# Decode attention with an MLP gate on one core: double K turns, one softmax pass per unit, and 640 rows of wo on eight partitions at a time

## The chip, the cores and the metric

The kernel runs on one core of a Trainium2 chip. The metric is the device time of one execution in microseconds (us). The core has five engines with their own instruction streams: TensorE (PE, matrix products; its weight loads are shown as PEld), VectorE (DVE), ScalarE (ACT), GpSimd (POOL) and SyncE (SP, which here only issues DMAs). Sixteen DMA engines move data between HBM and the on-chip memory SBUF. TensorE writes its results to PSUM.

## What is computed

One token of a decoder for a batch of two. Attention reads a cache of 32,768 keys and values for each of two sequences and eight KV heads; four query heads share one KV head. The attention output is projected by `wo` and multiplied by a gate that a small MLP makes from the same input.

```python
xn = layernorm(x)                                  # x: 2 x 1 x 512
q = (xn @ wq).reshape(B, 1, 32, 128)               # wq: 512 x 4096
scores = einsum("bhqd,bhkd->bhqk", q, k) * 128**-0.5   # K: 2 x 8 x 32768 x 128, bf16
p = softmax(scores)
o = einsum("bhqk,bhkd->bhqd", p, v)                # V: the same size as K
s = o.reshape(B, 1, 4096) @ wo                     # wo: 4096 x 512
h2 = gelu(layernorm(xn) @ w3) @ w4                 # the one token makes the rest of the MLP's
g = silu(xn + h2)                                  # first block zero
out = x + s * g
```

K and V together are 268 MB. Each element is used once or four times, so the kernel has to read all of it and does little with it.

## The kernel before

**Loads.** All large inputs go through five SBUF slots of 4 MB (`slots`, SLOTS = 5) in the order of the list `loads`: the first K chunk, wq, the second K chunk, w3, w4, and then K of unit n+1 and V of unit n by turns. A unit is one (sequence, KV head) pair; there are 16 units, and each has two K chunks and two V chunks (`NCH` = 2) of 16,384 rows. A chunk is one DMA of 128 partitions with 32 KB each. The main loop (line 441) walks the list, does the job of entry i, and then calls `issue(i + SLOTS)`, which starts the load five entries ahead on SP's queue. SP waits there until the slot is free. The last four entries are pieces of wo with 16, 8, 4 and 4 of the 32 rows that each partition holds (`wo_cuts`). The last V chunk is cut into two DMAs.

**K job** (`k_job`, line 295). A chunk is cut into eight blocks of 16 x 128 keys (`GT` = 16). For each block `transposed` turns 128 x 1024 words of 32 bits on VectorE in squares of 32 into a buffer `ktb` (`KTB` = 3 buffers), and `scores` then does four matmuls of 512 columns on the turned block. `scores` runs one block behind the turning (`LAG` = 1). The scores of a unit stand in two PSUM tiles `sc`, one for each half.

**Softmax.** After the last block of a half VectorE takes the maximum of that half (line 239), and after the second half the maximum of the two. The closures `step1` and `step2` are put on the list `glue` and run one after the other between later blocks: `step1` brings the maximum across partitions, `step2` does the exponential, its sum and a transposition (`pT`), each once per half.

**V job** (`v_job`, line 307). Each chunk takes 32 matmuls of 512 columns in four column strips of TensorE, all adding into `acc`. After a unit's last V chunk `unit_end` copies `acc` to SBUF, and its `step1` adds the four strips by `sel` in four fp32 products (`ot`, line 342), and writes the normalised output into `oQ` by four VectorE instructions of 32 partitions, so that one transposition (`oP`, line 354) has it ready for wo after the last head.

**wo job** (`wo_job`, line 358). For each of the 32 rows r of a partition it does four matmuls of 128 columns into four strips of `s_ps`, 128 matmuls in all. Two VectorE instructions (lines 458 and 460) then apply the gate and add x, and two DMAs store the result.

The instructions of each engine stand in the order in which the code issues them (`manual_schedule`); the framework adds the semaphore waits. The DMAs that SP issues use eight completion semaphores in rotation, and a DMA waits until the one eight places earlier has landed.

Of the kernel before, what the change touches and what calls it, by code (L numbers as in the profile page):

```python
# [8 lines left out]
F32 = mybir.dt.float32  # L9
BF16 = mybir.dt.bfloat16  # L10
U32 = mybir.dt.uint32
ACT = mybir.ActivationFunctionType
ALU = mybir.AluOpType
# [4 lines left out]
SLOTS = 5  # L18
KTB = 3
LAG = 1  # L20
# [3 lines left out]
def kernel(  # L24
# [44 lines left out]
    p_pool = ctx.enter_context(tc.tile_pool(name="prob", bufs=2))  # L69
    pt_pool = ctx.enter_context(tc.tile_pool(name="probT", bufs=4))  # L70
    tmp = ctx.enter_context(tc.tile_pool(name="tmp", bufs=3))
    sm_pool = ctx.enter_context(tc.tile_pool(name="small", bufs=3))
    sc_psp = ctx.enter_context(tc.tile_pool(name="sc_ps", bufs=4, space=bass.MemoryType.PSUM))
    acc_psp = ctx.enter_context(tc.tile_pool(name="acc_ps", bufs=1, space=bass.MemoryType.PSUM))
# [7 lines left out]
    NR = HD // 128  # L82
    wo_v = A_wo.rearrange("(p r) d -> p r d", r=NR)

# [3 lines left out]
    for n in range(NU):  # L88
        for c in range(NCH):
            if n + 1 < NU:  # L90
                loads.append(("K", n + 1, c))
            loads.append(("V", n, c))
    wo_cuts = [0, NR // 2, 3 * NR // 4, NR - 4, NR]
    loads += [("wo", r0, r1) for r0, r1 in zip(wo_cuts, wo_cuts[1:])]
    tiles = {}

    def issue(i):
        if i >= len(loads):
            return
        what = loads[i]  # L100
        t = slots.tile([128, UT * Dh], BF16, tag="slot", name=f"slot_{what[0]}")
        if what[0] in ("K", "V"):
            b, g = units[what[1]]
            c = what[2]
            src = A_k_cache if what[0] == "K" else A_v_cache
            sv = src[b, g, c * CH:(c + 1) * CH, :].rearrange("(p t) d -> p (t d)", p=128)
            w = UT * Dh // 2 if what == ("V", NU - 1, NCH - 1) else UT * Dh
            for w0 in range(0, UT * Dh, w):
                nc.sync.dma_start(out=t[:, w0:w0 + w], in_=sv[:, w0:w0 + w])
        elif what[0] == "wq":  # L110
            nc.sync.dma_start(
                out=t[:, 0:DK * HD].rearrange("p (k f) -> p k f", k=DK), in_=wq_v)
        elif what[0] == "wo":
            r0, r1 = what[1:]
            nc.sync.dma_start(
                out=t[:, 0:(r1 - r0) * D].rearrange("p (r d) -> p r d", d=D), in_=wo_v[:, r0:r1, :])
        elif what[0] == "w3":
            nc.sync.dma_start(
                out=t[:, 0:DK * Fdim].rearrange("p (k f) -> p k f", k=DK), in_=w3_v)
        else:  # L120
            nc.sync.dma_start(
                out=t[:, 0:FK * D].rearrange("p (f d) -> p f d", f=FK), in_=w4_v)
        tiles[what] = t
# [23 lines left out]
    for k in range(4):  # L147
        wb, par = k // 2, k % 2
        src = ident[:, :].rearrange("p (wb w two) -> p wb two w", wb=2, two=2)[:, wb, par, :]
        nc.vector.tensor_copy(out=pick[:, k, :, :], in_=src.unsqueeze(1).to_broadcast([128, 4, 32]))  # L150

    headm = pers.tile([128, rep], F32)
# [50 lines left out]
    oQ = pers.tile([128, B, NR], BF16)  # L203
    oP = pers.tile([128, B, NR], BF16)
    g_sb = pers.tile([B, D], F32)
# [8 lines left out]
    def state(n):  # L214
        if n not in unit_st:
            unit_st[n] = {
                "m2": sm_pool.tile([128, NHALF], F32, tag="m2", name="m2"),
                "sc": [], "pT": [],
            }
        return unit_st[n]  # L220

    def scores(n, grp, ktb):
        b, g = units[n]
        st = state(n)
        half, sl = grp // NS, grp % NS
        if sl == 0:
            st["sc"].append(sc_psp.tile([128, GT * 32], F32, tag="sc", name="sc"))
        sc = st["sc"][half]
        kv = ktb[:, :].bitcast(BF16).rearrange("p (t wb k two) -> p wb two t k", wb=2, k=32, two=2)
        off = 32 - rep - rep * sl  # L230
        for k in range(4):
            nc.tensor.matmul(  # L232
                sc[:, :].rearrange("p (t k) -> p t k", k=32),
                lhsT=qz[:, n % 2, k, off:off + 128],
                rhs=kv[:, k // 2, k % 2, :, :],
                start=(sl == 0 and k == 0), stop=(sl == NS - 1 and k == 3),
            )
        if sl == NS - 1:
            nc.vector.tensor_reduce(out=st["m2"][:, half:half + 1], in_=sc[:, :], axis=AX.X, op=ALU.max)  # L239
            if half == NHALF - 1:  # L240
                softmax_front(n)

    def softmax_front(n):
# [3 lines left out]
        m1 = sm_pool.tile([128, 1], F32, tag="m1", name="m1")  # L247
        nc.vector.tensor_reduce(out=m1[:, :], in_=st["m2"][:, :], axis=AX.X, op=ALU.max)  # L248

# [11 lines left out]
        def step2():  # L261
# [5 lines left out]
            nc.vector.tensor_scalar_mul(out=nb[:, :], in0=bc[:, :], scalar1=-inv_sqrt_dh)  # L267
            S2 = sm_pool.tile([128, NHALF], F32, tag="S2", name="S2")
            for hf in range(NHALF):
                pr = p_pool.tile([128, GT * 32], BF16, tag="p", name="pr")  # L270
                nc.scalar.activation(  # L271
                    out=pr[:, :], in_=st["sc"][hf][:, :], func=ACT.Exp,
                    bias=nb[:, 0:1], scale=inv_sqrt_dh, accum_out=S2[:, hf:hf + 1])
                pT = pt_pool.tile([128, GT, 32], BF16, tag="pT", name="pT")
                nc.vector.transpose(out=pT[:, :, :].rearrange("p t r -> p (t r)"), in_=pr[:, :])  # L275
                st["pT"].append(pT)
            S1 = sm_pool.tile([128, 1], F32, tag="S1", name="S1")
            nc.vector.reduce_sum(out=S1[:, :], in_=S2[:, :], axis=AX.X)
            Sm = sm_pool.tile([128, rep], F32, tag="Sm", name="Sm")
# [6 lines left out]
    def transposed(n, grp, kw):  # L286
        ktb = kt_pool.tile([128, GT * DW], U32, tag="ktb", name="ktb")
        nc.vector.transpose(out=ktb[:, :], in_=kw)  # L288
        waiting.append((n, grp, ktb))

    def flush(keep):
        while len(waiting) > keep:
            scores(*waiting.pop(0))

    def k_job(n, c):
        kw = tiles[("K", n, c)][:, :].bitcast(U32)
        for blk in range(NB):
            transposed(n, c * NB + blk, kw[:, blk * GT * DW:(blk + 1) * GT * DW])
            if n == 0 and c == 0 and blk < KTB:
                if blk == KTB - 1:  # L300
                    q_job()
                continue
            flush(LAG)
            if glue:
                glue.pop(0)()

    def v_job(n, c):
        vv = tiles[("V", n, c)][:, :].rearrange("p (e i t d) -> p e t i d", i=4, t=GT, d=Dh)
        for e in range(NB // 4):
            half, r0 = (c * NB + e * 4) // NS, (c * NB + e * 4) % NS * rep  # L310
            pT = unit_st[n]["pT"][half]
            for t in range(GT):
                j = t % 4
                nc.tensor.matmul(  # L314
                    acc[32 * j:32 * j + 16, :].rearrange("p (i d) -> p i d", d=Dh),
                    lhsT=pT[:, t, r0:r0 + 16],
                    rhs=vv[:, e, t, :, :],
# [14 lines left out]
    def unit_end(n):  # L332
# [5 lines left out]
        def step1():  # L338
# [7 lines left out]
            nc.vector.reciprocal(out=rc[:, :], in_=ot[:, rep:2 * rep])  # L346
            q0, c0 = g // 2 * 32, g % 2 * 4 * rep
            ov = oQ[q0:q0 + 32, b, c0:c0 + 4 * rep].rearrange("r (h a) -> r a h", a=4)
            for a in range(4):
                nc.vector.tensor_tensor(  # L350
                    out=ov[:, a, :], in0=ot[32 * a:32 * a + 32, 0:rep], in1=rc[32 * a:32 * a + 32, :],
                    op=ALU.mult)
            if g == Hkv - 1:
                nc.vector.transpose(out=oP[:, b, :], in_=oQ[:, b, :])

        glue.append(step1)

    def wo_job(r0, r1):
        w = tiles[("wo", r0, r1)]
        for r in range(r0, r1):  # L360
            for j in range(4):
                c0 = (r - r0) * D + 128 * j
                nc.tensor.matmul(
                    s_ps[32 * j:32 * j + B, :], lhsT=oP[:, :, r], rhs=w[:, c0:c0 + 128],
                    start=(r == 0), stop=(r == NR - 1), tile_position=(0, 32 * j))

# [74 lines left out]
    for i, what in enumerate(loads):  # L441
        if what[0] == "K":
            k_job(what[1], what[2])
        elif what[0] == "V":
            if what[2] == 0:
                while glue and len(unit_st[what[1]]["pT"]) < NHALF:
                    glue.pop(0)()
            v_job(what[1], what[2])
        elif what == ("w4",):
            mlp_job()  # L450
        elif what[0] == "wo":
            while glue:
                glue.pop(0)()
            wo_job(what[1], what[2])
        issue(i + SLOTS)
# [37 lines left out]
```

## Time and profile before

| | |
|---|---|
| median of 3 runs | 661.09 us (660.92 to 661.11) |
| profiled execution | 660.95 us, its span from first to last instruction 659.2 us |
| granted TensorE clock, mean | 0.794 of full speed |
| PE busy | 440.4 us (67%), 2594 matmuls |
| DVE busy | 391.0 us (59%), 551 instructions |
| ACT busy | 42.4 us (6%) |
| DMA | 280.89 MB, mean 426 GB/s; SP's queue 98.8% of 16 engines' span |
| K turns (line 288) | 256 instructions, 299.5 us, 1218 ns each |
| score matmuls (line 232) | 1024, 322.7 us, 461 ns each |
| V matmuls (line 314) | 1024, 68.9 us |

The page gives for each engine the time in which it was busy, a picture of the span in 40 slices, the DMA queues, the chain of waits that ended last, and the costliest groups of instructions. Windows of the trace give the same numbers for any stretch, with the granted clock and the share of the DMA engines that was busy; the timeline lists single instructions with what ended the idle time before them. Behind the DMA view the trace holds a record of every DMA packet with its start, duration, size and queue; it does not name the DMA engine.

### The profile page before, as it was taken

The page shows a single profiled execution, that of the slowest core. Times are in us where ns is not written, and L with a number is a line of the kernel's source. Part 1 is how long each engine was busy: PE and PEld are TensorE (multiplying, and loading weights), DVE is VectorE, ACT ScalarE, POOL GpSimd, SP SyncE. Part 2 cuts the span into 40 slices and gives each one's busy share as a digit, 9 for nine tenths or more (in the row PEclk, how much of TensorE's full clock was granted, in tenths as well). Part 3 has the DMA queues.
Part 4 walks back from the last instruction along what each step waited for, and adds up shares of the span by engine and source line. Part 5 has one row for each costly group of instructions (what it writes and reads, how often), then busy time and mean ns, then how long its engine had stood idle before and what let it go on. Part 6 is the DMA issues. An engine that isn't in the chain of part 4 may idle for free.

```text
span 659.2 us, 6264 instructions
## 1 busy us (share of the span) xinstructions
PE 440.4 (67%) x2594; PEld 183.1 (28%) x2594; DVE 391.0 (59%) x551; ACT 42.4 (6%) x136; POOL 2.2 (0%) x10
## 2 busy tenths in 40 slices
PE   0596968486685748757466885747678484965864
PEld 0342332132332213222122322213232221422233
DVE  6184957466664746657375765746576474666621
ACT  1103010000001000000100000000000000000000
POOL 1000000000000000000000000000000000000000
PEclk9997878879586886859788585977858788686976
DMA  9999999999999999999999999999999999999995
GB/s 382 420 436 439 427 437 430 430 442 420 440 430 430 440 424 436 435 425 439 427 435 435 424 442 428 431 439 425 437 433 429 441 423 436 430 430 440 430 422 245
DMA packets 10447, 280.89 MB, mean 426 GB/s; under 512 B 1194, under 2 KB 1204, under 8 KB 1460
## 3 DMA queue, kind: packets, MB, share of 16 engines
q1 hardware_dynamic: 10376, 280.50, 98.8%
q8 instruction: 20, 0.33, 0.2%
q14 instruction: 7, 0.06, 0.0%
q10 hardware_dynamic: 44, 0.01, 0.0%
HBM read 280.50 MB, written 0.00 MB: 426 GB/s over the span
## 4 chain that ended last, share of the span: by engine, by line
DMA 75%; PE 12%; DVE 8%; issue 4%; ACT 1%; SPq 0%; DVEq 0%; ACTq 0%
DMA slot_K<-in_A_k_cache_dram 39%; DMA slot_V<-in_A_v_cache_dram 30%; PE sc L232 7%; DVE ktb L288 6%; DMA slot_wq<-in_A_wq_dram 3%; PE acc L314 3%; DMA slot_wo<-in_A_wo_dram 2%; DVE pT L275 1%; PE h L425 1%; PE qT L372 1%; PE hT L405 1%; ACT pr L271 0%; DVE oQ L350 0%; PE ot L342 0%; PE bc L263 0%
## 5 line engine op out<-in xcount | busy, mean ns | idle before, releaser
L232 PE MATMUL sc<-ktb,qz 128*128 128x512 bf16 x1024 | 322.7, 461 | 169.9 <-DVE ktb L288 162.1
L288 DVE STREAM_TRANSPOSE ktb<-slot_K 128x1024 uint32<-128x1024 uint32 x256 | 299.5, 1218 | 121.2 <-DMA slot_K<-in_A_k_cache_dram 113.7
L232 PEld LDWEIGHTS <-qz 128*128 128x128 bf16 x1024 | 108.7, 112 | 350.8 <-issue 249.7
L314 PE MATMUL acc<-slot_V,pT 128*16 128x512 bf16 x1024 | 68.9, 391 | 13.9 <-DMA slot_V<-in_A_v_cache_dram 13.8
L239 DVE TENSOR_REDUCE m<-sc 128x1 f32<-128x512 f32 x32 | 22.1, 690 | 58.0 <-PE sc L232 58.0
L314 PEld LDWEIGHTS <-pT 128*16 128x16 bf16 x1024 | 24.0, 90 | 59.9 <-issue 40.0
L271 ACT ACTIVATE pr<-sc,nb 128x512 bf16<-128x512 f32 x32 | 21.7, 682 | 214.1 <-DVE nb L267 214.1
L396 ACT COPY qz<-qp 32x16 bf16<-32x16 bf16 x64 | 12.9, 201 | 343.2 <-PE sc L232 321.7
L275 DVE STREAM_TRANSPOSE pT<-pr 128x512 bf16<-128x512 bf16 x32 | 22.1, 711 | 14.4 <-ACT pr L271 14.4
L342 PE MATMUL ot<-sel,acs 128*128 128x4 f32 x128 | 25.5, 322 | 0.5 <-DVE acs L336 0.5
L342 PEld LDWEIGHTS ot<-sel,acs 128*128 128x128 f32 x128 | 24.9, 289 | 0.6 <-DVE acs L336 0.6
L336 DVE COPY acs<-acc 128x512 f32<-128x512 f32 x16 | 11.1, 692 | 17.6 <-PE acc L314 17.6
L372 PE MATMUL qT<-xT,slot_wq 128*128 128x2 bf16 x128 | 3.6, 165 | 12.4 <-DMA slot_wq<-in_A_wq_dram 12.4
L263 PEld LDWEIGHTS bc<-ones_f,gx 1*128 1x128 f32 x32 | 7.5, 291 | 13.4 <-issue 12.2
L350 DVE TENSOR_TENSOR oQ<-ot,rc 32x4 bf16<-32x4 f32 x64 | 10.5, 164 | 1.2
L267 DVE TENSOR_SCALAR nb<-bc 128x1 f32<-128x1 f32 x16 | 2.5, 155 | 14.5 <-PE bc L263 14.5
L340 PEld LDWEIGHTS ot<-Sm,ones_f 128*128 128x128 f32 x32 | 9.1, 291 | 6.2 <-issue 4.9
L263 PE MATMUL bc<-ones_f,gx 1*128 1x1 f32 x32 | 8.9, 344 | 1.1 <-DVE gx L257 1.1
L372 PEld LDWEIGHTS <-slot_wq 128*128 128x128 bf16 x128 | 3.5, 104 | 12.4 <-DMA slot_wq<-in_A_wq_dram 12.4
L346 DVE RECIPROCAL rc<-ot 128x4 f32<-128x4 f32 x16 | 2.4, 150 | 7.5 <-PE ot L342 7.5
L425 PE MATMUL h<-slot_w,h_bf 128*2 128x512 bf16 x14 | 5.4, 571 | 1.6 <-DVE h_bf L422 1.6
L252 PE MATMUL mT<-identf,m 128*1 128x128 f32 x16 | 4.3, 270 | 3.2 <-DVE m L248 3.2
(68 smaller groups left out, 69.0 us busy)
## 6 DMA issues: line engine op xcount, KB each, us to landing
slot_K<-in_A_k_cache_dram SPq DMA_DIRECT2D x32, 4096.0 KB, 40.0
slot_V<-in_A_v_cache_dram SPq DMA_DIRECT2D x31, 4096.0 KB, 34.0
slot_wq<-in_A_wq_dram SPq DMA_DIRECT2D x1, 4096.0 KB, 21.5
slot_V<-in_A_v_cache_dram SPq DMA_DIRECT2D x2, 2048.0 KB, 28.9
slot_w<-in_B_w_dram SPq DMA_DIRECT2D x2, 1792.0 KB, 39.2
slot_wo<-in_A_wo_dram SPq DMA_DIRECT2D x1, 2048.0 KB
slot_wo<-in_A_wo_dram SPq DMA_DIRECT2D x1, 1024.0 KB
slot_wo<-in_A_wo_dram SPq DMA_DIRECT2D x2, 512.0 KB, 13.4
```

What stands on the lines that cost most here:

```text
L232: nc.tensor.matmul(sc[:, :].rearrange("p (t k) -> p t k", k=32), lhsT=qz[:, n % 2, k, off:off + 128], rhs=kv[:, k // 2, k % 2, :, :], star ...
L239: nc.vector.tensor_reduce(out=st["m2"][:, half:half + 1], in_=sc[:, :], axis=AX.X, op=ALU.max)
L263: nc.tensor.matmul(bc[:, :], lhsT=st["gx"][:, :, :].rearrange("o x h -> o (x h)"), rhs=ones_f[0:1, 0:1], start=True, stop=True)
L271: nc.scalar.activation(out=pr[:, :], in_=st["sc"][hf][:, :], func=ACT.Exp, bias=nb[:, 0:1], scale=inv_sqrt_dh, accum_out=S2[:, hf:hf + 1])
L275: nc.vector.transpose(out=pT[:, :, :].rearrange("p t r -> p (t r)"), in_=pr[:, :])
L288: nc.vector.transpose(out=ktb[:, :], in_=kw)
L314: nc.tensor.matmul(acc[32 * j:32 * j + 16, :].rearrange("p (i d) -> p i d", d=Dh), lhsT=pT[:, t, r0:r0 + 16], rhs=vv[:, e, t, :, :], start ...
L336: nc.vector.tensor_copy(out=acs[:, :], in_=acc[:, :])
L342: nc.tensor.matmul(ot[:, 0:rep], lhsT=acs[:, i * Dh:(i + 1) * Dh], rhs=sel[:, i, :], start=(i == 0), stop=(i == 3))
L372: nc.tensor.matmul(qT_ps[:, h * B:(h + 1) * B], lhsT=w[:, k * HD + h * Dh:k * HD + (h + 1) * Dh], rhs=xT[:, k, :], start=(k == 0), stop=(k ...
L396: nc.scalar.copy(out=qz[32 * i:32 * i + 32, n % 2, :, c0:c0 + rep], in_=qp[32 * i:32 * i + 32, :, b, g, :])
L425: nc.tensor.matmul(h2_ps[0:B, :], lhsT=h_bf[:, f * B:(f + 1) * B], rhs=w4[:, f, :], start=(f == 0), stop=(f == FK - 1),)
```

## The change

K turns take two blocks at a time (`KG` = 2): one VectorE instruction of 128 x 2048 words into one of two buffers of double size. `scores` works on the halves of the buffer and stays two blocks behind. A unit's scores stand in one PSUM tile with both halves, so that maximum, exponential, sum and transposition are done once per unit over 1024 columns. `unit_end` writes `oQ` with one instruction of 128 partitions. In exchange `oQ` is no longer in the order that wo needs: the new `o_final` transposes both sequences at once, puts the rows in order with four matmuls against the permutation `perm`, and copies the result to `oP`, which now has four sections z.

wo comes in other pieces. Rows 0 to 26 of all 128 partitions come in three DMAs (16, 8 and 3 rows). Rows 27 to 31 (`RX` = 5), 640 rows of wo in all, come ahead of them into another slot by four DMAs of eight partitions each, four runs of 5,120 bytes per partition; they stand on partitions 0 to 31, with the quarter z along the free dimension. `wo_job` does these first, with 32 partitions at a time, 80 matmuls, and then 108 matmuls for rows 0 to 26.

In the built program VectorE's stream goes from 693 instructions, waits and others counted, to 404. TensorE's goes from 2498 matmuls to 2562.

```diff
-KTB = 3
+KTB = 2
+KG = 2
+RX = 5
...
-    sc_psp = ctx.enter_context(tc.tile_pool(name="sc_ps", bufs=4, space=bass.MemoryType.PSUM))
+    sc_psp = ctx.enter_context(tc.tile_pool(name="sc_ps", bufs=2, space=bass.MemoryType.PSUM))
...
-    wo_cuts = [0, NR // 2, 3 * NR // 4, NR - 4, NR]
-    loads += [("wo", r0, r1) for r0, r1 in zip(wo_cuts, wo_cuts[1:])]
+    RC = NR - RX
+    wo_cuts = [0, NR // 2, 3 * NR // 4, RC]
+    wo_x = A_wo.rearrange("(z q r) d -> q z (r d)", z=4, r=NR)
+    loads += [("wox",), ("wo",)]
...
+        elif what[0] == "wox":
+            for q0 in range(4):
+                nc.sync.dma_start(
+                    out=t[q0:32:4, 0:4 * RX * D].rearrange("p (z c) -> p z c", z=4),
+                    in_=wo_x[q0:32:4, :, RC * D:NR * D])
         elif what[0] == "wo":
-            r0, r1 = what[1:]
-            nc.sync.dma_start(
-                out=t[:, 0:(r1 - r0) * D].rearrange("p (r d) -> p r d", d=D), in_=wo_v[:, r0:r1, :])
+            for r0, r1 in zip(wo_cuts, wo_cuts[1:]):
+                nc.sync.dma_start(out=t[:, r0 * D:r1 * D], in_=wo_v[:, r0 * D:r1 * D])
...
+    perm = pers.tile([128, Hq, 4], BF16)
+    nc.vector.tensor_copy(out=perm[:, :, :], in_=ident[:, :].rearrange("p (a hh) -> p hh a", a=4))
...
-        if sl == NS - 1:
-            nc.vector.tensor_reduce(out=st["m2"][:, half:half + 1], in_=sc[:, :], axis=AX.X, op=ALU.max)
-            if half == NHALF - 1:
-                softmax_front(n)
+        if sl == NS - 1 and half == NHALF - 1:
+            softmax_front(n)
...
-            for hf in range(NHALF):
-                pr = p_pool.tile([128, GT * 32], BF16, tag="p", name="pr")
-                nc.scalar.activation(
-                    out=pr[:, :], in_=st["sc"][hf][:, :], func=ACT.Exp,
-                    bias=nb[:, 0:1], scale=inv_sqrt_dh, accum_out=S2[:, hf:hf + 1])
-                pT = pt_pool.tile([128, GT, 32], BF16, tag="pT", name="pT")
-                nc.vector.transpose(out=pT[:, :, :].rearrange("p t r -> p (t r)"), in_=pr[:, :])
+            pr = p_pool.tile([128, NHALF * GT * 32], BF16, tag="p", name="pr")
+            nc.scalar.activation(
+                out=pr[:, :], in_=st["sc"][:, :, :].rearrange("p x k -> p (x k)"), func=ACT.Exp,
+                bias=nb[:, 0:1], scale=inv_sqrt_dh, accum_out=S1[:, :])
+            pT = pt_pool.tile([128, NHALF * GT, 32], BF16, tag="pT", name="pT")
+            nc.vector.transpose(out=pT[:, :, :].rearrange("p t r -> p (t r)"), in_=pr[:, :])
...
-        ktb = kt_pool.tile([128, GT * DW], U32, tag="ktb", name="ktb")
+        ktb = kt_pool.tile([128, KG * GT * DW], U32, tag="ktb", name="ktb")
         nc.vector.transpose(out=ktb[:, :], in_=kw)
-        waiting.append((n, grp, ktb))
+        for x in range(KG):
+            waiting.append((n, grp + x, ktb[:, x * GT * DW:(x + 1) * GT * DW]))
...
-            for a in range(4):
-                nc.vector.tensor_tensor(
-                    out=ov[:, a, :], in0=ot[32 * a:32 * a + 32, 0:rep], in1=rc[32 * a:32 * a + 32, :],
-                    op=ALU.mult)
-            if g == Hkv - 1:
-                nc.vector.transpose(out=oP[:, b, :], in_=oQ[:, b, :])
+            nc.vector.tensor_tensor(
+                out=oQ[:, b, g * rep:(g + 1) * rep], in0=ot[:, 0:rep], in1=rc[:, :], op=ALU.mult)
...
+    def o_final():
+        nc.vector.transpose(
+            out=oT[:, :, :].rearrange("p b r -> p (b r)"), in_=oQ[:, :, :].rearrange("p b h -> p (b h)"))
+        op_ps = mi_psp.tile([128, 4, B * NR], F32, tag="mi", name="op")
+        pm = perm[:, :, :].rearrange("p h a -> p (h a)")
+        for z in range(4):
+            np = 128 if z == 0 else 32
+            nc.tensor.matmul(
+                op_ps[0:np, z, :], lhsT=pm[:, 32 * z:32 * z + np],
+                rhs=oT[:, :, :].rearrange("p b r -> p (b r)"), start=True, stop=True)
+        nc.vector.tensor_copy(out=oP[:, 0, :, :].rearrange("p b r -> p (b r)"), in_=op_ps[:, 0, :])
+        nc.vector.tensor_copy(
+            out=oP[0:32, 1:4, :, :].rearrange("p z b r -> p z (b r)"), in_=op_ps[0:32, 1:4, :])
+
+    def wo_job():
+        w, wx = tiles[("wo",)], tiles[("wox",)]
+        parts = [(32, z, RC + i, wx, z * RX + i) for z in range(4) for i in range(RX)]
+        parts += [(128, 0, r, w, r) for r in range(RC)]
+        for i, (kp, z, r, t, c) in enumerate(parts):
             for j in range(4):
-                c0 = (r - r0) * D + 128 * j
+                c0 = c * D + 128 * j
                 nc.tensor.matmul(
-                    s_ps[32 * j:32 * j + B, :], lhsT=oP[:, :, r], rhs=w[:, c0:c0 + 128],
-                    start=(r == 0), stop=(r == NR - 1), tile_position=(0, 32 * j))
+                    s_ps[32 * j:32 * j + B, :], lhsT=oP[0:kp, z, :, r], rhs=t[0:kp, c0:c0 + 128],
+                    start=(i == 0), stop=(i == len(parts) - 1), tile_position=(0, 32 * j))
```

## The prediction

> **What bounds the kernel now.** I read the page's head, its slices and DMA queues first.
>
> ```profile
> span 659.2 us, 6264 instructions
> ...
> DMA  9999999999999999999999999999999999999995
> ...
> q1 hardware_dynamic: 10376, 280.50, 98.8%
> q8 instruction: 20, 0.33, 0.2%
> q14 instruction: 7, 0.06, 0.0%
> ...
> DMA 75%; PE 12%; DVE 8%; issue 4%; ACT 1%; SPq 0%; DVEq 0%; ACTq 0%
> ```
>
> SP's queue holds the 16 DMA engines for 98.8% of the span, and only the last slice (16.5 us) shows a gap. No cheaper compute can shorten the first 640 us; what is open is the end. The timeline there:
>
> ```profile
> 645.29 1.04 PE L314 MATMUL acc<-slot_V,pT 128*16 128x512 bf16 x16 [2.07 <-DMA slot_V<-in_A_v_cache_dram]
> ...
> 647.12 1.87 PE L342 MATMUL ot<-sel,acs 128*128 128x4 f32 x8 [0.47 <-DVE acs L336]
> ...
> 649.25 0.70 DVE L350 TENSOR_TENSOR oQ<-ot,rc 32x4 bf16<-32x4 f32 x4
> 649.98 0.21 DVE L354 STREAM_TRANSPOSE oP<-oQ 128x32 bf16<-128x32 bf16 x1
> ...
> 650.25 1.88 PE L363 MATMUL s_ps<-slot_wo,oP 128*2 128x128 bf16 x64 [1.26 <-DVE oP L354]
> ...
> 655.02 0.60 PE L363 MATMUL s_ps<-slot_wo,oP 128*2 128x128 bf16 x16 [0.64 <-DMA slot_wo<-in_A_wo_dram]
> ```
>
> Two chains start from the last V piece at 645.29: compute up to oP (650.25) with the wo matmuls behind it, and the rest of wo by DMA, whose last piece lets the last 16 matmuls go at 655.02. Windows (busy time of PE, PEld, DVE, ACT, POOL, then granted clock, DMA share, GB/s):
>
> ```profile
> 649.00:650.00 1.00, 0.00 (x0) 0.00 (x0) 0.86 (x6) 0.00 (x0) 0.00 (x0) 0.50 0.96 401
> 650.00:651.00 1.00, 0.75 (x32) 0.75 (x36) 0.20 (x1) 0.00 (x0) 0.00 (x0) 0.50 0.75 311
> 651.00:652.00 1.00, 1.00 (x44) 0.93 (x33) 0.00 (x0) 0.00 (x0) 0.00 (x0) 0.50 0.55 229
> 652.00:653.00 1.00, 0.54 (x28) 0.41 (x23) 0.00 (x0) 0.00 (x0) 0.00 (x0) 0.50 0.62 246
> 653.00:654.00 1.00, 0.82 (x36) 0.63 (x28) 0.00 (x0) 0.00 (x0) 0.00 (x0) 0.50 0.30 123
> 654.00:655.00 1.00, 0.38 (x16) 0.19 (x5) 0.00 (x0) 0.00 (x0) 0.00 (x0) 0.50 0.13 53
> ```
>
> From 650 the DMA engines fall out one after the other: equal loads end up to 4.6 us apart. The packet records show why. In SP's queue each engine moves its packets without a gap (32,768 bytes each 1.210 us, 16,384 each 0.608, 4,096 each 0.156). An instruction packet delays the one engine that carries it. The twenty 16,384-byte packets of q8 fit TensorE's stream (some 5,200 records) and fall by turns on eight engines, 1.42 us each time. Five of the seven 8,192-byte packets of q14 fall on one engine, call it X, outside those eight, 0.84 us each; they come at some 57 VectorE records and then every 120 to 150. wo's last completions: seven engines 650.12 to 650.93, X 654.52, the eight 652.91 to 654.72.
>
> **The change, part by part.** I work against the profiled execution (660.95 us: span 659.18 and 1.77 around it) and put the difference on the median of the runs, 661.09. About 0.2%, 1.3 us, is what a measurement of this kernel can tell from no change.
>
> *K turns.* 256 turns at 1.15 to 1.22 us become 128 at about 2.3. The first refill that waits for a turn is issued at 36.81 us, while the engines are served until 49.6; a doubled turn ends at most one block (1.2 us) and one pair of score blocks (3.6 us) later, so 11 us of cover shrink to 6 or more. Later loads are issued 34 to 40 us ahead of landing. With the clock at half, a K job's 32 score matmuls and a V job's 32 take some 13.7 and 3.4 us of the 19.4 us in which their two chunks arrive. Cost nothing, covered by the queue.
>
> *Softmax.* Per unit two maxima of 0.69 us, two exponentials of 0.68 and two transpositions of 0.69 become one each of about twice the length; three small instructions go. In the last unit this chain ends at 633.4, and V lands at 635.6. Nothing; 2.2 us of cover.
>
> *SP.* Seven wo issues stand where four stood (0.33 us each). Their added waits, in the rotation of semaphores, are for K and V chunks; the last piece, behind all others, waits for the first half of the last V chunk, landed by 640.5, and the engines reach it after 650. Nothing.
>
> *wo's bytes.* Each engine loses two pieces of eight 4,096-byte packets (2.49 us) and gets one of eight 3,072-byte packets: on the straight line through the durations above, 4.8 ns plus 0.0368 ns per byte, 0.118 us each, 0.94. So 1.55 us less. The four small DMAs have one partition per engine and four packets of 5,120 bytes each (0.193 us): 16 packets and four completions, 3.11 us more on eight engines, net +1.56. Which eight? In the trace the x loads of four partitions fell on four engines, X among them and none of the q8 eight. I take it that eight partitions take these four and the other four outside q8.
>
> *VectorE's stream.* 693 instructions become 404, so fetches at about 57, 185 and 313 remain and two of five go: X gains 1.69 us. Then the seven end at 651.7 to 652.5, X at 654.52 + 1.56 - 1.69 = 654.39, the others at 651.4 to 653.17. wo's last piece lands 0.33 us earlier, not 1.5, since X carries most of it. For the two lost fetches bounds are 0 and 1.69.
>
> The Trainium skill (Runtime: NRT & Kernel Launch, Instruction fetch mechanics) says that refills come in 16 KiB blocks of 256 instructions. q8's 16,384-byte packets agree, q14's 8,192 bytes do not. By the page VectorE's 289 instructions fewer are one fetch, X would end at 655.23, and the last matmuls would start about 0.5 us later than before.
>
> *o_final.* oQ takes one instruction in place of four: the transposition starts at 649.46 in place of 649.98 and, 128x64, lasts between the 0.21 of 128x32 and the 0.69 of 128x512, about 0.25. PE starts 0.06 later, 649.76. Four matmuls of 64 columns: line 381 has the same shape, 0.41 us to the next VectorE start at full clock; at half clock I take 0.55 (bounds 0.4 and 0.8). The first copy is the cast of line 378, 0.22; PE starts wo at 650.58. The second copy (under 0.42) lies under the first 20 matmuls. So 0.33 us later than before.
>
> *wo matmuls.* 188 in place of 128. The 64 of line 363 go out four per 106.6 ns at clock 0.50, 26.7 each. From 650.58 the last starts 187 x 26.7 ns = 4.98 later, at 655.56; in the trace it was 655.31. All pieces are there: wox by 646.2 on X, the 16 rows by 651.0, the 8 rows by 653.5, and the 3 rows at 654.39 + 0.30 = 654.69, when PE comes to them at 655.28. So before, PE waited for wo; now wo is there and PE is late: +0.25 us.
>
> The clock sets the size. With the 8 fp32 matmuls of ot at full clock (1.03 us in unit 14 at 602.27, 1.87 here) PE is 0.84 earlier and wo's landing holds it: last start 654.69 + 11 x 26.7 ns = 654.98, -0.33. With the V matmuls at 645.29 at half clock (four in 427 ns at 639 to 642) they take 0.75 more: 656.31, +1.0.
>
> The Trainium skill (TensorE: Matmul & The Clock Gate, Part 1) says that an idle window of about 3.4 us halves the clock and a busy one restores it. It speaks against work added right behind a wait, as here; a full busy window inside the 5 us would take perhaps 0.5 off (an estimate from that page).
>
> **The rivals.**
>
> *The lightened engines are the wrong ones (slower).* Everything rests on which engines take the eight-partition DMAs and on X's fetches. If X keeps its five fetches, it ends at 656.08, the last matmul starts 656.08 + 0.30 + 0.29 = 656.67: +1.36, 662.45. If the small DMAs fall on the q8 engines: 654.72 + 1.56 = 656.28, last start 656.87, +1.56, 662.65. It decides once any engine ends after 654.98 (PE's arrival at 655.28 less 0.30). For it: X is one engine and the trace names none. Against: the four x packets.
>
> *The end is evened out (faster).* If X loses four fetches it ends at 652.7, and the q8 engines at 653.17 set the landing; with PE ready as well (ot at full clock, starting at 649.7, and matmuls at half their time, 2.5 us), the last start is 653.17 + 0.30 + 0.15 = 653.62: -1.69, 659.4. Against: all windows from 647 on show 0.50, and the 128 small matmuls of line 372 took 28 ns each (3.59 us) even at full clock.
>
> *The stream breaks (slower).* If two double buffers leave VectorE and PE waiting for each other so long that a slot comes free over 11 us late at the head, SP's queue runs dry; a K job's added wait of one block pair, 3.6 us, once, gives 664.7. Against: issue-to-landing times of 34 to 40 us.
>
> **How the numbers follow.** Forecast, PE's tail takes the place of wo's DMA wait: 0.70, 661.09 + 0.25 = 661.3, own range 660.8 to 662.1. Wrong engines: 0.18, 662.4 to 662.7. Evened out: 0.07, 659.4. Stream: 0.05, 664.7. The range 660.6 to 662.6 takes in the forecast and most of the first rival. Faster 0.08, same 0.70, slower 0.22: the forecast lies within 0.2%, the rivals outside it.
>
> **What would show it.** Right: DMA slices full up to 645; the wait for the last V piece ending at 645.3 again; some 313 VectorE instructions on the page and two packets fewer in q14; 188 wo matmuls from 650.6 without a wait for slot_wo; DMA share falling later but to zero before PE's end. Wrong: a wait of PE on slot_wo at the end (X or the q8 engines late), the wo matmuls at another pace than 26.7 ns, the last V piece landing at another time, or SP's loads issued late at the head.

## The result, and the profile after

| | before | after |
|---|---|---|
| median | 660.92 us (660.81 to 661.20, 13 runs) | 662.36 us (661.28 to 663.07, 13 runs) |
| profiled execution | 660.95 us, span 659.2 | 662.72 us, span 660.8 |
| ratio after/before | | 1.0019 (1.0011 to 1.0026) |

The change costs 1.4 us between the medians. That is inside the predicted range (660.6 to 662.6) and, by the ratio, right at the 0.2% up to which the prediction spoke of no change. But the forecast itself was +0.25 us with an own range of 660.8 to 662.1, and the median lies above that, just under the first rival's 662.4 to 662.7. The whole range holds only because it was drawn over part of that rival. After also scatters more: its runs lie 1.8 us apart, those of before 0.4.

First the head, the slices, the DMA queues, the chain and two groups from the page of after.

```profile
span 660.8 us, 6068 instructions
...
PE 421.8 (64%) x2658; PEld 175.5 (27%) x2658; DVE 365.4 (55%) x313; ACT 38.5 (6%) x104; POOL 2.3 (0%) x10
...
DMA  9999999999999999999999999999999999999994
...
q1 hardware_dynamic: 10392, 280.50, 98.6%
q8 instruction: 21, 0.34, 0.2%
q14 instruction: 5, 0.04, 0.0%
...
DMA 68%; PE 18%; DVE 10%; issue 2%; ACT 1%; SPq 0%; DVEq 0%; ACTq 0%
...
L294 DVE STREAM_TRANSPOSE ktb<-slot_K 128x2048 uint32<-128x2048 uint32 x128 | 292.0, 2298 | 169.7 <-DMA slot_K<-in_A_k_cache_dram 142.1
...
L256 DVE TENSOR_REDUCE m<-sc 128x1 f32<-128x1024 f32 x16 | 19.5, 1222 | 29.9 <-PE sc L242 29.9
```

VectorE's part did what it says: 313 instructions for 551, two packets fewer in q14, 25 us less work. Nothing of it reaches the end, because the DMA row is full up to the last slice, as before. What happened at the end must be read from the timeline. Each line there has the start, the busy time, the instruction group, and in brackets the idle time before it with what ended it.

```profile
645.38 1.89 PE L321 MATMUL acc<-slot_V,pT 128*16 128x512 bf16 x16 [3.05 <-DMA slot_V<-in_A_v_cache_dram]
...
648.06 1.87 PE L349 MATMUL ot<-sel,acs 128*128 128x4 f32 x8 [0.27 <-DVE acs L343]
...
650.19 0.16 DVE L354 TENSOR_TENSOR oQ<-ot,rc 128x4 bf16<-128x4 f32 x1
650.38 0.25 DVE L360 STREAM_TRANSPOSE oT<-oQ 128x64 bf16<-128x64 bf16 x1
650.68 0.48 PE L366 MATMUL op<-oT,perm 128*128 128x64 bf16 x4 [0.75 <-DVE oT L360]
...
651.48 2.30 PE L380 MATMUL s_ps<-slot_wox,oP 32*2 32x128 bf16 x80 [0.32 <-DVE oP L369]
...
653.71 3.40 PE L380 MATMUL s_ps<-slot_wo,oP 128*2 128x128 bf16 x108
...
657.22 0.29 DVE L476 TENSOR_TENSOR sg<-s_ps,g 128x128 f32<-128x128 f32 x1 [5.54 <-issue]
```

The last V piece lands at 645.38, where before had 645.29. Everything up to there is unchanged. The 16 V matmuls then take 1.89 us instead of 1.04, and the wo matmuls start at 651.48 instead of 650.25. The 108 matmuls look like one run without a wait, but they are not. The windows of one microsecond (columns as in the prediction: busy time of PE with its count, ..., granted clock, DMA share, GB/s) show it:

```profile
654.00:655.00 1.00, 1.00 (x48) 1.00 (x44) 0.00 (x0) 0.00 (x0) 0.00 (x0) 0.50 0.17 70
655.00:656.00 1.00, 0.89 (x40) 0.70 (x32) 0.00 (x0) 0.00 (x0) 0.00 (x0) 0.50 0.11 46
656.00:657.00 1.00, 1.00 (x40) 0.73 (x30) 0.00 (x0) 0.00 (x0) 0.00 (x0) 0.50 0.09 19
```

At 655 the count falls below the steady pace (40 for 48), and at 655 and 656 DMA engines are still moving data (shares 0.11 and 0.09 of sixteen: about two engines). In before the last wo packets had landed by 654.72. The instruction records have two stops inside the run of 108: the matmul at 655.70 comes 0.32 us late, the one at 656.62 0.11 us late. They are the 65th and the 97th of the 108, the first of the 8-row piece and the first of the 3-row piece, so these are waits for wo. The last matmul starts at 656.80, in before at 655.31: +1.49 us, and the span is 1.6 us longer.

So two chains end close together here. Without its two stops TensorE would have started its last matmul at 656.80 - 0.32 - 0.11 = 656.37, already 1.06 later than before. And wo's last piece, by the packet records, landed at 656.23, 1.51 later than before; with the 0.57 us from there to the start of the last matmul (656.80) it is the later of the two in this execution. The experiments take the two apart.

wo's last completions by DMA engine, put together from the packet records by following each engine's packets, which stand end to start:

| engines | before | after |
|---|---|---|
| X, which carries VectorE's packets | 654.52 | 654.49 |
| three that carry three of TensorE's 16,384-byte packets until then | 654.51, 654.59, 654.72 | 653.17; with the four small DMAs besides, 656.03 and 656.23 |
| the other twelve | 650.12 to 653.45 | 648.82 to 652.59 |

The two late engines can be found in the other runs too. In every run in which the small DMAs come in packets that can be followed, TensorE's packets up to 640 us take 0.88 to 0.89 us each on these two, and 0.92 or more on the other six of its eight engines. In before the two with 0.88 stand fifth and sixth in the rotation; they carry two packets and end at about 652.9 and 653.2. In after they stand second and third and carry three. So their 3 us are one packet more (1.42) and the small DMAs (1.56): where the rotation starts counts as much as the small DMAs do.

### The profile page after: what moved, and what is told of

It reads as the page before. It is cut to its first block, busy times and chain, and to the rows that moved or that the text cites. A ratio compares the mean times of both kernels' runs of the same rounds, so it can differ in the third digit from the quotient of the medians.

```text
span 660.8 us, 6068 instructions
## 1 busy us (share of the span) xinstructions
PE 421.8 (64%) x2658; PEld 175.5 (27%) x2658; DVE 365.4 (55%) x313; ACT 38.5 (6%) x104; POOL 2.3 (0%) x10
## 4 chain that ended last, share of the span: by engine, by line
DMA 68%; PE 18%; DVE 10%; issue 2%; ACT 1%; SPq 0%; DVEq 0%; ACTq 0%
DMA slot_K<-in_A_k_cache_dram 56%; PE sc L242 12%; DVE ktb L294 8%; DMA slot_V<-in_A_v_cache_dram 7%; DMA slot_wq<-in_A_wq_dram 3%; PE acc L321 3%; DMA slot_wo<-in_A_wo_dram 2%; ACT pr L279 1%; DVE pT L283 1%; PE h L442 1%; PE qT L389 1%; PE hT L422 1%; PE bc L272 0%; DVE m L256 0%; DVE nb L276 0%
## 5 line engine op out<-in xcount | busy, mean ns | idle before, releaser
L242 PE MATMUL sc<-ktb,qz 128*128 128x512 bf16 x1024 | 310.3, 459 | 198.7 <-DVE ktb L294 197.0
L294 DVE STREAM_TRANSPOSE ktb<-slot_K 128x2048 uint32<-128x2048 uint32 x128 | 292.0, 2298 | 169.7 <-DMA slot_K<-in_A_k_cache_dram 142.1
L242 PEld LDWEIGHTS <-qz 128*128 128x128 bf16 x1024 | 110.5, 111 | 368.7 <-issue 304.7
L256 DVE TENSOR_REDUCE m<-sc 128x1 f32<-128x1024 f32 x16 | 19.5, 1222 | 29.9 <-PE sc L242 29.9
L283 DVE STREAM_TRANSPOSE pT<-pr 128x1024 bf16<-128x1024 bf16 x16 | 19.9, 1245 | 21.2 <-ACT pr L279 21.2
L279 ACT ACTIVATE pr<-sc,nb 128x1024 bf16<-128x1024 f32 x16 | 17.8, 1113 | 234.0 <-DVE nb L276 234.0
L349 PE MATMUL ot<-sel,acs 128*128 128x4 f32 x128 | 18.2, 265 | 0.3 <-DVE acs L343 0.3
L349 PEld LDWEIGHTS ot<-sel,acs 128*128 128x128 f32 x128 | 17.2, 209 | 0.4 <-DVE acs L343 0.4
L347 PEld LDWEIGHTS ot<-Sm,ones_f 128*128 128x128 f32 x32 | 6.2, 203 | 3.8 <-issue 1.7
```

Source lines behind the costliest of these rows:

```text
L242: nc.tensor.matmul(sc[:, half, :].rearrange("p (t k) -> p t k", k=32), lhsT=qz[:, n % 2, k, off:off + 128], rhs=kv[:, k // 2, k % 2, :, :] ...
L256: nc.vector.tensor_reduce(out=m1[:, :], in_=st["sc"][:, :, :].rearrange("p x k -> p (x k)"), axis=AX.X, op=ALU.max)
L279: nc.scalar.activation(out=pr[:, :], in_=st["sc"][:, :, :].rearrange("p x k -> p (x k)"), func=ACT.Exp, bias=nb[:, 0:1], scale=inv_sqrt_dh ...
L349: nc.tensor.matmul(ot[:, 0:rep], lhsT=acs[:, i * Dh:(i + 1) * Dh], rhs=sel[:, i, :], start=(i == 0), stop=(i == 3))
```

## The experiments

The theory after this reading: the loss sits in the wo part alone. It has two ends, wo's landing on two engines that take both kinds of load, and TensorE's longer tail, and the later one counts. The rivals: the doubled K turns cost something after all; the tail alone explains it; the landing alone explains it. Ratios are against runs of the kernel before on the same chip, with 95% intervals. The edits are shortened and, unless said otherwise, shown against the kernel after.

**1. K turns and softmax alone.** Of the change only the VectorE part is kept:

```diff
-RX = 5
...
-    wo_cuts = [0, NR // 2, 3 * NR // 4, RC]
-    loads += [("wox",), ("wo",)]
+    wo_cuts = [0, NR // 2, 3 * NR // 4, NR - 4, NR]
+    loads += [("wo", r0, r1) for r0, r1 in zip(wo_cuts, wo_cuts[1:])]
```

(`unit_end` and `wo_job` also as before.)

> K turns of two blocks and one softmax pass per unit, with wo, unit_end and wo_job as in the kernel before. Two ends compete (theory): the end is the later of wo's last landing and of TensorE's chain behind the last V piece, and neither is touched here except that the engine with VectorE's instruction packets is relieved: 660.8 to 661.1 us, no change. Rival, the doubled turns or the longer softmax steps cost time by themselves: +0.5 to +1.4 us.

Measured: 660.99 us (660.81 to 661.38) against 660.96, ratio 1.0001 (0.9992 to 1.0010). The last lines of its timeline are those of before:

```profile
645.15 1.22 PE L310 MATMUL acc<-slot_V,pT 128*16 128x512 bf16 x16 [2.38 <-DMA slot_V<-in_A_v_cache_dram]
...
654.88 0.60 PE L359 MATMUL s_ps<-slot_wo,oP 128*2 128x128 bf16 x16 [0.63 <-DMA slot_wo<-in_A_wo_dram]
```

VectorE is busy for 373.4 us here, 17.6 less than in before. The stream of K and V is not touched by the doubled turns: V lands at 645.15. X is relieved (its wo ends at 653.16, from 654.52), and it brings nothing, since three engines with three of TensorE's packets end at 654.46 to 654.51. The rival "the stream breaks" is gone, and so is any gain from fewer VectorE fetches as long as those engines stand.

**2. The wo part alone.** The new pieces of wo, `o_final` and the 188 matmuls; K turns and softmax as before.

```diff
-KTB = 2
-KG = 2
+KTB = 3
...
-        for blk in range(0, NB, KG):
-            transposed(n, c * NB + blk, kw[:, blk * GT * DW:(blk + KG) * GT * DW])
+        for blk in range(NB):
+            transposed(n, c * NB + blk, kw[:, blk * GT * DW:(blk + 1) * GT * DW])
```

> wo in pieces, o_final and 188 wo matmuls as in the kernel after, K turns and softmax as before (VectorE 647 instructions). Theory of two ends: five instruction packets stay on VectorE's DMA engine, which with the eight-partition DMAs ends wo near 656.1, as two other engines do: 661.3 to 662.8 us, median 662.3 to 662.5, a little or nothing above the kernel after. Rival, the loss comes from VectorE's new form: 660.9.

Measured: 662.65 us (662.39 to 663.06), ratio 1.0026 (1.0016 to 1.0036): the whole loss, and a little more than was expected.

```profile
650.76 2.30 PE L384 MATMUL s_ps<-slot_wox,oP 32*2 32x128 bf16 x80 [0.32 <-DVE oP L373]
...
653.19 1.88 PE L384 MATMUL s_ps<-slot_wo,oP 128*2 128x128 bf16 x64
655.62 1.41 PE L384 MATMUL s_ps<-slot_wo,oP 128*2 128x128 bf16 x44 [0.54 <-DMA slot_wo<-in_A_wo_dram]
```

TensorE starts 0.72 earlier than in after and waits the more: 0.54 us for slot_wo, named. In the packet records X keeps its five fetches here and ends at 656.18; the two engines with both loads end at 655.95 and 656.15. With X late in every execution there is no early one: the lowest of its 8 runs is 662.39, that of after 661.28.

**3. The small DMAs on all sixteen engines.** If the extra load on eight engines is the matter, one DMA of 32 partitions should spread it.

```diff
-            for q0 in range(4):
-                nc.sync.dma_start(
-                    out=t[q0:32:4, 0:4 * RX * D].rearrange("p (z c) -> p z c", z=4),
-                    in_=wo_x[q0:32:4, :, RC * D:NR * D])
+            nc.sync.dma_start(
+                out=t[0:32, 0:4 * RX * D].rearrange("p (z c) -> p z c", z=4),
+                in_=wo_x[:, :, RC * D:NR * D])
```

> As the kernel after, but the 640 rows come by one DMA of 32 partitions, two for each of 16 DMA engines, in place of four DMAs of eight. Theory of two ends: wo lands as before (654.7 in the profile), TensorE's 188 matmuls and o_final stay, so the end is TensorE's: +0.2 to +1.2 us over the kernel before by the clock at the last V matmuls, median 661.4 to 661.9; no wait of TensorE for slot_wo. Rival, only the unevenly loaded DMA engines cost: 660.9. Rival, they cost nothing: 662.4 as the kernel after.

Measured: 667.01 us (666.71 to 667.18), ratio 1.0090 (1.0077 to 1.0104). That is a clear miss: 6 us slower, where less than 1 was expected. The reason stands ahead of wo:

```profile
649.61 1.88 PE L320 MATMUL acc<-slot_V,pT 128*16 128x512 bf16 x16 [6.58 <-DMA slot_V<-in_A_v_cache_dram]
```

The last V piece lands at 649.61 instead of 645.4. It stands ahead of the small DMA in SP's queue. But the engines are not in step: in after the first is through with V at 640.4 and turns to the small DMAs, the last at 644.9. In this run packets run slow and overlap each other from 640.5 on: the 5,120-byte ones mostly 0.3 to 0.6 us (0.19 in after) and the 16,384-byte ones mostly 0.8 to 1.3 (0.608). These windows of this run (granted clock, DMA share and GB/s at the end) have engines busy and little moved:

```profile
636.00:640.00 4.00, 4.00 (x34) 2.75 (x30) 0.34 (x2) 0.00 (x0) 0.00 (x0) 0.50 1.06 446
...
642.00:644.00 2.00, 1.03 (x12) 0.27 (x5) 0.00 (x0) 0.00 (x0) 0.00 (x0) 0.78 1.04 251
...
646.00:648.00 2.00, 0.00 (x0) 0.00 (x0) 0.00 (x0) 0.00 (x0) 0.00 (x0) 0.57 0.92 127
```

The share stays near 1 while the rate falls from 446 to 127 GB/s. Why the packets slow down is not shown by this run. So spreading is not the remedy in this form, and it says nothing on the question that it was sent for.

**4. No small DMAs.** All 32 rows come on 128 partitions in the pieces of before; `o_final` stays, with 128 matmuls.

```diff
-RX = 5
+RX = 0
...
-    wo_cuts = [0, NR // 2, 3 * NR // 4, RC]
-    loads += [("wox",), ("wo",)]
+    wo_cuts = [0, NR // 2, 3 * NR // 4, NR - 4, NR]
+    loads += [("wo",)]
```

> As the kernel after, but all 32 rows of wo on 128 partitions in four DMAs of 16, 8, 4 and 4 rows as before: o_final stays, 128 wo matmuls. Theory of two ends: wo lands as before at 654.7, TensorE starts wo at 650.6 to 651.5 and would be through at 654.0 to 654.9, ahead of the last piece: 660.8 to 661.1 us. Rival, o_final lies on the path: +0.3 us, 661.2 to 661.3.

Measured: 660.85 us (660.66 to 661.29), ratio 0.9999 (0.9990 to 1.0007).

```profile
645.16 1.89 PE L321 MATMUL acc<-slot_V,pT 128*16 128x512 bf16 x16 [2.84 <-DMA slot_V<-in_A_v_cache_dram]
...
651.26 3.16 PE L380 MATMUL s_ps<-slot_wo,oP 128*2 128x128 bf16 x112 [0.32 <-DVE oP L369]
654.87 0.51 PE L380 MATMUL s_ps<-slot_wo,oP 128*2 128x128 bf16 x16 [0.45 <-DMA slot_wo<-in_A_wo_dram]
```

TensorE starts wo as late as in after (V matmuls at half the clock, `o_final` in front), and still waits 0.45 us for the last piece. With wo's loads as before there was 1 us of idle time to swallow `o_final` and the slow clock. The loss lies in the small DMAs and what they demand: transfers, or 60 more matmuls.

**5. TensorE's part by itself.** Experiment 4 with 60 matmuls more, of 32 partitions as in after, into a PSUM tile that nothing reads; the transfers are those of before.

```diff
+        scr = mi_psp.tile([128, 128], F32, tag="mi", name="scr")
+        for i in range(15):
+            for j in range(4):
+                nc.tensor.matmul(
+                    scr[32 * j:32 * j + B, :], lhsT=oP[0:32, 0, :, i], rhs=w[0:32, i * D + 128 * j:i * D + 128 * j + 128],
+                    start=(i == 0), stop=(i == 14), tile_position=(0, 32 * j))
```

> e4 (wo on 128 partitions by four DMAs, o_final) with 60 matmuls of 32 partitions ahead of the 128, into a PSUM tile that nobody reads: TensorE's end of the kernel after without its transfers. Theory of two ends: wo lands at 654.5 to 654.7, TensorE starts at 650.6 to 651.5 by the clock, and 188 matmuls of 26.7 ns bring the last start to 655.6 to 656.5, against 655.3 before: +0.2 to +1.2 us, median 661.3 to 662.0. Rival, the transfers alone make the loss: 660.9. Rival, TensorE alone makes it: 662.4.

Measured: 661.86 us (661.47 to 663.03) against 660.98, ratio 1.0015 (1.0007 to 1.0024). The tail alone costs 0.9 us. Of this 0.7 lies in the span from first to last instruction (659.8 for 659.1 us, medians); the rest lies outside it (2.06 for 1.82), and no trace shows why.

```profile
645.21 1.04 PE L321 MATMUL acc<-slot_V,pT 128*16 128x512 bf16 x16 [2.19 <-DMA slot_V<-in_A_v_cache_dram]
...
650.46 1.76 PE L380 MATMUL scr<-slot_wo,oP 32*2 32x128 bf16 x60 [0.32 <-DVE oP L369]
...
652.16 3.66 PE L386 MATMUL s_ps<-slot_wo,oP 128*2 128x128 bf16 x128
```

The profiled execution (661.50 us, the second fastest of its runs) is the tail that the prediction forecast: V matmuls at full clock, 188 matmuls from 650.46 without a wait, the last one starting at 655.51, 0.20 after before's 655.31. The other runs are up to 1.5 us longer.

**6. The same with the clock kept up.** Matmuls of a tile of zeros, 44 in TensorE's wait for the last V piece and 6 on either side of the four fp32 products, go into a PSUM tile ahead of its real use; `fill(x)` issues x of them. The edit is against experiment 5.

```diff
+            if n == NU - 1 and c == NCH - 1 and e == 0:
+                fill(44)
...
+            if n == NU - 1:
+                fill(6)
             for i in range(4):
...
+            if n == NU - 1:
+                fill(6)
```

> e5 with filler matmuls by zeros into s_ps, before wo's first product overwrites it: 44 while the last half of V is awaited, 6 while acc is copied, 6 after ot. If the spread and part of the loss of e5 come from the clock, which falls to half when TensorE waits for V, the clock stays at full up to ot and TensorE starts wo by 650.0 or earlier: the end goes back to wo's landing, 660.8 to 661.0 us, runs close together. Rival, the clock does not matter here: as e5, or up to 1 us later where the filler itself runs at half clock.

Measured: 661.09 us (660.92 to 661.54), ratio 1.0003 (0.9994 to 1.0012): 0.77 us less than experiment 5 on the same chip (0.5 of it in the span, 0.27 outside), and the scatter shrinks from 1.6 to 0.6 us. The median is 0.1 above the 660.8 to 661.0 that were expected.

```profile
645.30 1.04 PE L321 MATMUL acc<-slot_V,pT 128*16 128x512 bf16 x16
...
647.14 1.05 PE L362 MATMUL ot<-sel,acs 128*128 128x4 f32 x8
...
650.13 1.76 PE L395 MATMUL scr<-slot_wo,oP 32*2 32x128 bf16 x60 [0.78 <-DMA slot_wo<-in_A_wo_dram]
```

Windows of experiment 5 and then of this one, two microseconds each, with the granted clock third from the end:

```profile
647.00:649.00 2.00, 1.87 (x8) 1.81 (x9) 0.05 (x1) 0.00 (x0) 0.00 (x0) 0.50 0.97 408
```

```profile
647.00:649.00 2.00, 1.48 (x16) 1.29 (x15) 0.68 (x4) 0.00 (x0) 0.00 (x0) 1.00 0.97 410
```

The fp32 products take 1.05 us in place of 1.87, and `oP` is ready 0.8 us sooner. Now TensorE waits for wo again, at its start and, by the instruction records, for 0.2 us at the last piece (654.99). Its last matmul starts at 655.27, in before at 655.31: the end is back at wo's landing. The clock falls at 649.17 here (0.58 in the window from 649), so the wo matmuls from 650.13 run at 0.50 all the same.

When does the clock fall? These windows show it, two of before and then two of after:

```profile
644.00:646.00 2.00, 0.71 (x16) 0.31 (x15) 0.00 (x0) 0.00 (x0) 0.00 (x0) 1.00 1.01 430
646.00:647.00 1.00, 0.65 (x10) 0.30 (x2) 0.62 (x1) 0.00 (x0) 0.00 (x0) 0.75 0.94 401
```

```profile
643.00:645.00 2.00, 0.00 (x0) 0.00 (x0) 0.00 (x0) 0.00 (x0) 0.00 (x0) 0.94 1.04 442
645.00:647.00 2.00, 1.62 (x16) 0.43 (x15) 0.00 (x0) 0.00 (x0) 0.00 (x0) 0.50 1.03 440
```

A mean of 0.75 from 646 to 647 is a fall from 1.00 to 0.50 at 646.50, behind the 16 V matmuls (645.29 to 646.33, 1.04 us); 0.94 from 643 to 645 is a fall at 644.75, ahead of them (1.89 us). The clock records behind the windows say the rest. In all runs the granted clock is 1.00 or 0.50 and changes only at whole multiples of 3.41 us from one change to the next, and the place of this grid varies between executions. Near the end the clock is full for one stretch: 643.08 to 646.50 in before and in experiment 5, 641.33 to 644.75 in after, 641.51 to 644.93 in experiment 4. In experiment 6 the filling goes with two such stretches, 642.34 to 649.17. The wait for V does not decide it by its length. It is longer in after (3.05 us for 2.07) because the full clock came earlier and the 40 V matmuls ahead of it took 3.59 us for 4.44; the same stretch then ended before V landed.

The Trainium skill (TensorE: Matmul & The Clock Gate, Part 1) puts the halving at an idle window of about 3.4 us. The length of the stretches agrees; none of them was wholly idle (in before it held the 1.04 us of V matmuls).

**7. The transfers by themselves.** All transfers of after, but the products of the quarters z = 1 to 3 are not made, so that 128 matmuls remain.

```diff
-        parts = [(32, z, RC + i, wx, z * RX + i) for z in range(4) for i in range(RX)]
+        parts = [(32, z, RC + i, wx, z * RX + i) for z in range(1) for i in range(RX)]
```

> The kernel after with the products of quarters z = 1 to 3 of rows 27 to 31 left out (60 matmuls; the transfers stay): the transfers' end without TensorE's. TensorE would be through by 654 to 655 at 128 matmuls. Theory of two ends: wo's last piece lands with 656.2 on the engines that carry both TensorE's instruction packets and the eight-partition DMAs, last matmuls 656.6: 662.0 to 662.5 us, and 661.0 to 661.4 in executions where these packets fall on other engines. Rival, only TensorE's matmuls and o_final make the loss: 660.9.

Measured: 662.38 us (660.96 to 662.85), ratio 1.0018 (1.0009 to 1.0026). The transfers alone cost 1.4 us.

```profile
650.73 0.70 PE L380 MATMUL s_ps<-slot_wox,oP 32*2 32x128 bf16 x20 [0.32 <-DVE oP L369]
...
653.05 1.88 PE L380 MATMUL s_ps<-slot_wo,oP 128*2 128x128 bf16 x64 [1.62 <-DMA slot_wo<-in_A_wo_dram]
...
655.50 1.43 PE L380 MATMUL s_ps<-slot_wo,oP 128*2 128x128 bf16 x44 [0.57 <-DMA slot_wo<-in_A_wo_dram]
```

TensorE, relieved of 60 matmuls, waits for the first piece (1.62 us), for the second (0.57) and shortly for the third. Its last matmul starts at 656.61, nearly as late as in after.

Its eleven runs fall into two heaps, three at 660.96 to 661.15 and eight at 662.24 to 662.85. In the packet records of this run the two engines with both loads were the first and the eighth in the rotation by which TensorE's packets go round eight engines (with three packets and two); in after and in experiment 2 they were the second and the third. So the rotation starts on another engine in another execution. With three packets here an engine ends at about 656.1, with two at 654.57. Four more profiled executions of the same kernel were to pair time and rotation.

> The kernel without the products of z = 1 to 3 again, one look, to pair an execution's time with the engines that TensorE's instruction packets of 16,384 bytes fall on. Theory (the starting place in the rotation sets the time): a look near 662.4 us shows one of the two engines that carry both the four small DMAs and these packets with three packets, ending wo at 656.0 to 656.2; a look near 661.0 shows both with two packets at most, their ends at 654.6 or below. Rival (V's landing or the clock sets it): the times differ with the wait for the last V piece ending earlier or later than 645.1 to 645.4, and the two engines' packets do not follow the time.

> As in the look before: three packets on an engine of the small DMAs and about 662.4, or two at most and about 661.0 (theory); or no such pairing (rival).

> As in the look before: three packets on an engine of the small DMAs and about 662.4, or two at most and about 661.0 (theory); or no such pairing (rival).

> As in the look before: three packets on an engine of the small DMAs and about 662.4, or two at most and about 661.0 (theory); or no such pairing (rival).

Measured: 662.56, 662.31, 662.51 and 662.62 us, beside 660.82 of before. In all four the two engines were the first and the second in the rotation, with three packets each, and wo ended on them at 656.15, 655.93, 656.16 and 656.11. V landed at 645.2 to 645.4 in all, and the V matmuls took 1.04, 1.88, 1.04 and 1.66 us without effect on the order of the times, so neither moves this kernel out of the late heap. The pairing holds on the late side in five executions. No execution near 661.0 was profiled, so that the early heap is one with two packets on both engines remains argued, not shown. That such starts occur is shown by before (fifth and sixth): there the small DMAs would bring these two to 653.2 + 1.56 = 654.8, an estimate, about where wo lands in before (654.72).

## Why the prediction was right or wrong

*The bound.* Right. DMA slices are full to 645, V lands at 645.1 to 645.4 in all kernels but experiment 3, and experiment 1 shows that 17.6 us less on VectorE are worth nothing (ratio 1.0001).

*VectorE's stream and X.* Right: three fetches at 70.6, 289.2 and 522.4 us, five packets in q14, and X's wo ended at 654.49 where the sum gave 654.39.

*Which engines take the small DMAs.* This step failed: "I take it that eight partitions take these four and the other four outside q8." The four small DMAs fell on X and its three neighbours of the x loads, as said, but of the other four two belong to the eight that carry TensorE's packets. An engine with three such packets, at 654.5 to 654.7 before, plus the sum's own 1.56 gives 656.1 to 656.3; 656.03 and 656.23 were measured. The price was right and stood in the first rival, "the small DMAs fall on the q8 engines", with its last start at 656.87 (measured 656.80). Its chance of 0.18 rested on that one assumption, for which the trace of before had four packets of x and no more. The trace could have bounded it: sixteen engines less eight of q8 leave eight, and that the eight used are just these was one choice among many. The price also needs three of TensorE's packets on one of the two, and the sum took the counts of one execution as fixed; they go with the start of the rotation, which the prediction did not consider. That the median still fell into the stated range is owed to the range, not to the mechanism of the forecast.

*wo's start.* 650.58 was said and 651.48 measured. `o_final` was well sized: from oQ's start to the first wo matmul it took 651.48 - 650.19 = 1.29 us (1.00 before; the sum had 0.33 more, the trace has 0.29). The rest is the clock. That the V matmuls could run at half clock stood there as a bound, "they take 0.75 more: 656.31, +1.0"; they took 0.85 more, and without its stops TensorE's last matmul would have started at 656.37. The forecast took the clock of the one profiled execution as fixed. The runs show that it is not: the full stretch of 3.41 us ended at 646.50 in before and at 644.75 in after, behind the same 16 matmuls and ahead of them. In after this did not set the end, since wo's landing came later still.

*Pace.* Right: four matmuls in 106.7 ns at half clock, those of 32 partitions as well. The step from 32 to 128 partitions cost one gap of 0.24 us in place of about 0.10.

*"PE's tail takes the place of wo's DMA wait."* Half right. Experiment 5 shows the mechanism by itself (+0.9 on the medians, +0.20 in the last start where the clock was up), and in experiment 6, with the clock up, nothing measurable is left of it (ratio 1.0003, 0.9994 to 1.0012). But experiment 7 shows that wo was not there in time, so the wait did not go; it moved to two other engines. Gains and losses do not add: +0.9 and +1.4 alone, +1.44 together, since the later end counts.

*Where the relief went.* The small DMAs only shift load: 1.55 us off eight engines, net 1.56 onto the other eight. Of those, X had its two lost fetches to set against it, five had 3.8 us or more to spare (650.93 and earlier, where the end was at 654.72), and two carry TensorE's packets: with two of them there are 1.5 us to spare, with three next to nothing. The end is the latest engine's.

## What to carry to other kernels

When a queue keeps sixteen DMA engines busy to the end, work out the end per engine, and before extra transfers are put on some of them, find in a short trial which engines a DMA of that many partitions takes and which already carry instruction packets, in more than one execution; spread over disjoint partitions alone does not tell. Work that is added behind a wait of 2 to 3 us on TensorE should be priced at full and at half clock, since either held here from one execution to the next. 56 matmuls of zeros in and around the wait took 0.77 us off experiment 5; in the kernel after, where wo's landing sets the end, they were not tried. Neither the VectorE part alone nor the change without its small DMAs beat the kernel before measurably (660.99 and 660.85 against 660.96).

## What the hardware showed that was not expected

- One DMA of 32 partitions on sixteen engines, within a stream of 128-partition DMAs, cost 6 us, while the same bytes as four DMAs of eight partitions with a step of 4 kept each packet at its 0.19 us. The Trainium skill (DMA: Bandwidth & Descriptors, The descriptor swizzle) has each of the sixteen engines write its own set of eight partitions in a 128-partition transfer, and one section earlier (Back-pressure in remote DMA, on transfers between cores) says that a saturated destination port holds up the engines that share the path. The slow packets and the fall to 127 GB/s would fit that: sixteen engines on the 32 partitions that belong to eight. No run here shows the ports, and a 32-partition DMA on other partitions was not tried.
- The rotation of TensorE's instruction packets over eight DMA engines does not start on the same engine in each execution: of the two engines that also carried the small DMAs, one was first and the other second in four executions, first and eighth in one, second and third in two. Where all engines have equal loads this matters little, since some engine always has three packets; before scatters by 0.4 us. With unequal loads it does.
- TensorE's granted clock changed on a grid of 3.41 us in all 13 profiled executions, and the place of the grid varied, so the same 16 matmuls at the same time took 1.04 us in one execution and 1.89 in another.
